# A fused scan, SwiGLU and softplus kernel: another preparation of its first four units

## The chip, the cores and the metric

The kernel runs on one core of one Trainium2 chip. The metric is the device time of one execution in microseconds (us). TensorE is called PE here, VectorE DVE, ScalarE ACT, GpSimd POOL; SP is the engine that issues nearly all transfers.

## The reference

A chunked linear-attention scan runs over 4 batches of 8 heads and 768 positions; its output (3072 tokens of 256 values) goes through a root-mean-square norm and a SwiGLU MLP of width 1536, and then through a softplus MLP of width 2048. All of it is float32.

```python
for c in range(nc):                       # 24 chunks of 32 positions
    cum = np.cumsum(la, axis=-1)
    L = np.exp(cum[:, :, :, None] - cum[:, :, None, :]) * causal
    M = np.einsum('bhin,bhjn->bhij', Cc, Bc) * L
    y[:, :, sl] = M @ xc + (Cc @ state) * np.exp(cum)
    state = decay_full * state + sum_j(Bc xc decay_from_j)
...
xn = x / rms * rms_g
x = ((g := xn @ w_gate) * sigmoid(g) * (xn @ w_val)) @ w_out     # 256 -> 1536 -> 256
h = x @ w_in
return softplus(h) @ w_out2                                      # 256 -> 2048 -> 256
```

## The kernel before

**Units.** The scan is cut into 24 units of 128 positions, one for each batch and stretch: units 0 to 3 are the first stretch of the four batches, 4 to 7 the second. A unit (function `unit`) first makes its decays: two DVE scans of 128x512 (line L505) that multiply up the values of `a`, which every partition must hold. For a "spread" unit PE copies them to all partitions with four small matmuls (`p<-Sm,ident`); for the others a transfer of 512 KB does it (`ab<-a_clip`, L465; units 2 and 3 of the first block use the tiles `xxh` and `xxl` as their decay buffers, so there the name is `xxh<-...`, `xxl<-...`). `a_clip` is a clipped copy of `a` that the kernel itself writes to DRAM at the start (L778). Then PE computes the scores (`a<-hw`), DVE multiplies them into the decays (L552, two of 128x512) and scales B (L525), and PE applies the result (`t<-xc`, `t<-ab,xc`; from unit 4 on also `a<-xc,Sm` for the carried state, for which DVE multiplies in the products of the decays, L519). ACT drains the output into `xxh` (squares) and `xxl`; `norm` averages the squares on PE (`p<-mean,xxh`), takes the root on POOL, spreads it with PE (`p<-ident,rs`), and DVE applies it (L661) and takes the rest after rounding (L306, 128x256).

**The MLPs.** Tokens go in 6 blocks of 512 (4 units). Each float32 product is made of three matmuls of 128x512: high weight times high value, high times low, low times high. `front1` makes one of 12 slices of the gate (`wg`) and of the value (`wv`), 6 matmuls each; ACT applies silu (L706), DVE multiplies (L710), ACT rounds (`hw`), DVE takes the rest (L306, `hw<-s,hw`); `back` multiplies the slice by `wo` (`t<-hw,woh`). The second MLP has 16 slices with `wi` and `wp`.

**Weights.** 34 chunks of 512 KB of packed weights arrive in three rotating buffers `wr`. Each needs an ACT conversion (`zz`, L389), a DVE shift and merge (L391), an ACT rounding to the high part (L394), and the rest, the low part: on DVE (L396), but for the first four chunks (`PE_RESTS`) by PE, two products with scaled identities (`p<-wr,wil` and, for instance, `p<-wgh,wil`) that ACT then copies out (L299).

**Order.** All operations are collected in a plan with a rank and a cost; `Plan.emit` then walks through time and always emits the operation that can start first, on any engine, with ties going to the lower rank. That fixes each engine's instruction order; on the chip every engine runs its list strictly in that order and waits by semaphores. 40 idle matmuls (`p<-mean`, "fillers") have the lowest rank after the first eight. Transfers on SP reuse eight semaphores in turn, so each also waits for the eighth one before it.

Of the kernel before, what the change touches and what calls it, by code (L numbers as in the profile page):

```python
# [13 lines left out]
ACTF = mybir.ActivationFunctionType  # L14
# [3 lines left out]
P = 128  # L18
# [5 lines left out]

BLOCKS = [4, 4, 4, 4, 4, 4]

NATIVE, SPREAD = 8, 4
NORMS = {0: [1, 1, 1, 1]}

EARLY, HEAD = 2, 2  # L30
# [6 lines left out]

LAT, DMA_LAT = 300, 500

ANY_ORDER = {}  # L40

PE_RESTS, REST_LEAD = 4, 6
F1 = 1536 // P
F2 = 2048 // P
KD = DM // P
# [17 lines left out]
class Plan:  # L63
# [48 lines left out]
    def emit(self):  # L112
# [57 lines left out]
        while len(order) < n:  # L170
            best = None
            for e in engines:
                able = []
                for i in cand[e]:
                    t = start(i, e)
                    if t is not None:
                        able.append((t, ops[i][1], i))
                while able:
                    t, rank, i = min(able)
                    if best is not None and t >= best[0]:  # L180
                        break
                    end = t + ops[i][0][e][0]

                    later = False
                    for e2, way in ops[i][0].items():
                        if e2 != e:
                            ns, t2 = way[0], start(i, e2)
                            t2 += sum(ops[j][0][e2][0] for j in cand[e2]
                                      if len(ops[j][0]) == 1 and ops[j][1] < rank and ready[j] <= t2)
                            later = later or t2 + ns < end  # L190
                    if not later:
                        best = (t, e, i)
                        break
                    able.remove((t, rank, i))
            if best is None:
                raise RuntimeError("no operation can run")
            t, e, i = best
            ns, fn, *shared = ops[i][0][e]
            for e2 in ops[i][0]:
                cand[e2].discard(i)  # L200
            end = t + ns
            if e == "pe":
                end = self.clock(t, ns, ops[i][4], ticks)
            if e in dma:

                dma[e] = max(t + 1100, dma[e]) + ns * (1.5 if e == "actq" else 1.0)
                end = dma[e] + DMA_LAT
                free[e] = t + 475
            else:
                free[e] = end  # L210
                if e == "pool":
                    port = end
            order.append(fn)
            for key, b in news[i]:
                slots[key].remove(min(slots[key]))
                taken[key].add(b.turn)
                while first[key] in taken[key]:
                    first[key] += 1
            for b in uses[i]:
                b.left -= 1  # L220
                b.rel = max(b.rel, end + self.latency)
                if not b.left:
                    slots[b.pool, b.tag].append(b.rel)
            for j, data in succ[i]:
                if data:
                    ready[j] = max(ready[j], end + (20 if list(ops[j][0]) == [e] else self.latency))
                left[j] -= 1
                if not left[j]:
                    enter(j)
# [5 lines left out]
def tile_ssd_then_swiglu_then_softplus_mlp(  # L235
# [34 lines left out]
    def f32(t):  # L270
        return t.bitcast(F32)
# [16 lines left out]
    def DVE(n, rank, fn, r=(), w=(), fast=False, port=True, ns=None):  # L288
        plan.op({"dve": (ns or dve_ns(n, fast), fn) + (("port",) if port else ())}, rank, r, w)
# [71 lines left out]
    for i in range(F2 // 2):  # L361
        chunks += [("wi", i), ("wp", i)]


    MINUS, minus = len(chunks) - 2, "minus"

    def scaled_ident():
        return W["wi"][1][:, F2 - 1]

    def weight(c):  # L370
        nm, i = chunks[c]
        b0 = blocks[0]
# [19 lines left out]
            op0=ALU.logical_shift_right, op1=ALU.bitwise_or), [raw, zk], [raw])  # L392
        h, l = (W[nm][s][:, 2 * i:2 * i + 2].rearrange("p a k f -> p (a k f)") for s in (0, 1))
        ACT(n, rank, lambda: act.activation(out=h, in_=r(), func=ACTF.Copy, scale=256.0), [raw], [(nm, i, 0)])  # L394
        if c >= PE_RESTS:
            DVE(n, rank, lambda: dve.scalar_tensor_tensor(out=l, in0=r(), scalar=256.0, in1=f32(h), op0=ALU.mult,  # L396
                op1=ALU.subtract), [raw, (nm, i, 0)], [(nm, i, 1)] + [minus] * (c == MINUS))
            return
        gp = pbuf("p", [P, 4 * P])

        def rest():
            mm(gp(), f32(scaled_ident()[:, 0]), r(), True, False)
            mm(gp(), scaled_ident()[:, 1], h, False, True)
        PE(1090, use - REST_LEAD, rest, [raw, (nm, i, 0), "ident", minus], [gp], 2560)
        COPY(n, rank, lambda: l, gp, [gp], [(nm, i, 1)], False)

    wp = []

# [32 lines left out]
    def unit(u):  # L441
# [83 lines left out]
                dve.tensor_tensor(out=ob, in0=ob, in1=lst.to_broadcast([P, NH, NS]), op=ALU.mult)  # L525
            DVE(128, rank[0], scale, [(abt, 0), (abt, 1), xbt], [(xbt, "b")])
        nxt(2)
        gps = [pbuf("a", [P, 4 * P]) for _ in range(2)]
        if nat:

            def scores():
# [229 lines left out]
    with tc.manual_schedule():  # L761
# [2 lines left out]
        ACT(384, -101, lambda: act.activation(  # L764
            out=ident4[:, P:4 * P].rearrange("p (o i) -> p o i", o=3),
            in_=ident.rearrange("p (o i) -> p o i", o=1).to_broadcast([P, 3, P]), func=ACTF.Copy), ["eye"], ["ident"])
        for k, m in enumerate((256.0, -1.0)):
            ACT(128, -50, lambda k=k, m=m: act.activation(out=scaled_ident()[:, k], in_=ident, func=ACTF.Copy, scale=m), ["ident"], [minus])

        def a_view(t):  # L770
            return t.rearrange("u o (h g i) -> (u o h) g i", g=2, i=P)

# [124 lines left out]
```

## Time and profile before

| | |
|---|---|
| median of 3 runs | 652.39 us (652.33 to 652.45) |
| the profiled execution: its time, its span | 651.48 us, 649.0 us |
| PE busy | 643.7 us, 99% of the span |
| DVE busy | 339.7 us, 52%; by tenths nearly full up to 130 us |
| ACT busy | 309.9 us, 48% |
| POOL busy | 24.6 us, 4% |

Before the first matmul of the MLP (`p<-xxh,wgh`, at 34.99 us) PE carries the first units and the fillers; from there to the end it carries the MLPs, with the later units in between. An operation that waits shows the engine and line that released it in brackets.

### The profile page before, as it was taken

How to read it: one execution, taken by the hardware profiler on the slowest of the kernel's cores; microseconds unless marked ns; L12 is line 12 of the kernel's file. 1: busy time of each engine (PE TensorE's matmuls, PEld its weight loads, DVE VectorE, ACT ScalarE, POOL GpSimd, SP SyncE). 2: the span in 40 equal slices, each digit the busy share in tenths (PEclk: the TensorE clock that was granted, in tenths of full speed). 3: DMA queues.
4: the chain of work that ended last, by engine and by line, in shares of the span. 5: the costliest groups of instructions: out<-in, count | busy, mean ns of one | idle time of the engine just before them, and what ended most of it. 6: DMA issues, size and time to landing. Idle time of an engine off the chain costs nothing.

```text
span 649.0 us, 9018 instructions
## 1 busy us (share of the span) xinstructions
PE 643.7 (99%) x3492; PEld 528.9 (81%) x3492; DVE 339.7 (52%) x566; ACT 309.9 (48%) x547; POOL 24.6 (4%) x32
## 2 busy tenths in 40 slices
PE   9999999999999999999999999999999999999997
PEld 7778888888888888888888888888888888887785
DVE  5988988876833237564324963423753422233321
ACT  4376657756355444233643433644432544433543
POOL 1210000000100001000001100000000000000000
PEclk9999999999999999999999999999999999999999
DMA  6786776574500015300323420141500000000000
GB/s 209 223 292 195 241 273 197 196 230 165 172 1 32 2 32 171 123 1 0 123 89 124 140 62 1 70 141 32 171 1 1 1 1 0 33 1 0 1 1 32
DMA packets 36777, 61.36 MB, mean 95 GB/s; under 512 B 3424, under 2 KB 18304, under 8 KB 36736
## 3 DMA queue, kind: packets, MB, share of 16 engines
q1 hardware_dynamic: 36304, 59.23, 28.0%
q10 hardware_dynamic: 432, 1.57, 0.7%
q8 instruction: 27, 0.44, 0.3%
q14 instruction: 14, 0.11, 0.1%
HBM read 47.58 MB, written 13.21 MB: 94 GB/s over the span
## 4 chain that ended last, share of the span: by engine, by line
PE 98%; ACT 0%; DVE 0%; issue 0%; DVEq 0%
PE p L268 55%; PE t L268 36%; PE a L268 8%; DVE hw L306 0%; ACT hw L299 0%; DVE xxl L751 0%; DVE s L710 0%; ACT s L722 0%; ACT xxh L299 0%; ACT s L756 0%; DVE mean L781 0%; DVE small L782 0%; DVEq L710 0%
## 5 line engine op out<-in xcount | busy, mean ns | idle before, releaser
L306 DVE TENSOR_TENSOR hw<-s,hw 128x512 fp32r<-128x512 f32 x162 | 113.5, 703 | 179.6 <-ACT hw L299 178.9
L299 ACT ACTIVATE hw<-s 128x512 fp32r<-128x512 f32 x162 | 101.9, 632 | 99.5 <-DVE s L710 76.8
L268 PE MATMUL t<-hw,wph 128*128 128x512 f32 x384 | 119.6, 392 | 0.2 <-DVE hw L306 0.2
L722 ACT ACTIVATE s<-p 128x512 f32<-128x512 f32 x96 | 56.9, 598 | 103.7 <-PE p L268 102.6
L710 DVE TENSOR_TENSOR s<-s,p 128x512 f32<-128x512 f32 x72 | 49.2, 683 | 72.7 <-PE p L268 65.4
L268 PEld LDWEIGHTS t<-hw,wph 128*128 128x128 f32 x384 | 71.3, 188 | 16.7 <-issue 1.2
L268 PE MATMUL t<-hw,woh 128*128 128x512 f32 x264 | 82.3, 392 | 0.4 <-DVE hw L306 0.2
L268 PE MATMUL p<-xxl,wih 128*128 128x512 f32 x192 | 74.9, 390 | 0.2 <-DVE xxl L751 0.2
L268 PE MATMUL p<-xxh,wih 128*128 128x512 f32 x192 | 75.0, 390 | 0.0
L268 PE MATMUL t<-hw,wpl 128*128 128x512 f32 x192 | 74.7, 389 | 0.0
L268 PE MATMUL p<-xxh,wil 128*128 128x512 f32 x192 | 74.7, 389 | 0.0
L706 ACT ACTIVATE s<-p 128x512 f32<-128x512 f32 x72 | 43.0, 597 | 62.9 <-PE p L268 61.5
L268 PEld LDWEIGHTS t<-hw,woh 128*128 128x128 f32 x264 | 49.2, 188 | 11.7 <-DVE hw L306 0.8
L268 PE MATMUL p<-xxh,wgh 128*128 128x512 f32 x144 | 57.1, 397 | 0.0
L268 PE MATMUL p<-xxh,wvh 128*128 128x512 f32 x144 | 57.0, 396 | 0.0
L268 PE MATMUL p<-xxl,wgh 128*128 128x512 f32 x144 | 56.2, 390 | 0.0
L268 PE MATMUL p<-xxh,wvl 128*128 128x512 f32 x144 | 56.1, 390 | 0.0
L268 PE MATMUL p<-xxl,wvh 128*128 128x512 f32 x144 | 56.1, 390 | 0.0
L268 PE MATMUL p<-xxh,wgl 128*128 128x512 f32 x144 | 56.1, 389 | 0.0
L505 DVE TENSOR_TENSOR_SCAN ab<-ab,ident 128x512 f32<-128x512 f32 x40 | 50.4, 1279 | 5.8 <-DMA ab<-a_clip 5.8
L268 PE MATMUL t<-hw,wol 128*128 128x512 f32 x132 | 51.4, 389 | 0.0
L268 PEld LDWEIGHTS p<-xxl,wih 128*128 128x128 f32 x192 | 36.1, 188 | 8.0 <-DVE xxl L751 0.7
(121 smaller groups left out, 782.1 us busy)
## 6 DMA issues: line engine op xcount, KB each, us to landing
wr<-in_w SPq DMA_DIRECT2D x31, 512.0 KB, 4.3
ab<-a_clip SPq DMA_DIRECT2D x20, 512.0 KB, 4.5
parts<-wr SPq DMA_DIRECT2D x16, 512.0 KB, 3.6
xc<-in_xc SPq DMA_DIRECT2D x20, 256.0 KB, 4.4
st<-parts SPq DMA_DIRECT2D x16, 256.0 KB, 3.1
cz<-parts SPq DMA_DIRECT2D x32, 128.0 KB, 3.8
out_y<-s SPq DMA_DIRECT2D x12, 256.0 KB, 2.9
wr<-in_bc SPq DMA_DIRECT2D x8, 256.0 KB, 3.3
```

The source lines that it names most:

```text
L268: pe.matmul(out=o, lhsT=l, rhs=r, start=start, stop=stop, skip_group_check=True)
L299: ways = {"act": (act_ns(n), lambda: act.activation(out=out(), in_=in_(), func=ACTF.Copy)), "dve": (dve_ns(n, sbuf), lambda: dve.tensor_co ...
L306: return lambda: eng.tensor_tensor(out=out(), in0=in_(), in1=f32(hi()), op=ALU.subtract)
L505: DVE(512, rank[0], lambda t=t, d=d: dve.tensor_tensor_scan(out=t(), data0=d(), data1=ident4, initial=0.0, op0=ALU.mult, op1=ALU.add), dk ...
L706: ACT(n, rank - EPI, lambda: act.activation(out=s()[:, 0:n], in_=ps[0]()[:, 0:n], func=ACTF.Silu), [ps[0]], [s, "table"] if new_table else ...
L710: DVE(n, rank - EPI, lambda: dve.tensor_tensor(out=s()[:, 0:n], in0=s()[:, 0:n], in1=ps[1]()[:, 0:n], op=ALU.mult), [s, ps[1]], [s], port= ...
L722: ACT(n, rank - EPI, lambda: act.activation(out=s()[:, 0:n], in_=hp()[:, 0:n], func=ACTF.Softplus), [hp], [s, "table"] if new_table and f ...
```

## The change

Four things change. `SPREAD` goes from 4 to 2: the decays of units 2 and 3 come by transfer from `a_clip`. The scores of units 1 and 3 go into banks of the pool `p` of PSUM, which the MLP uses, instead of `a`. `PE_RESTS` is gone: the low parts of all chunks are made by DVE, and the scaled identities are not built. And `emit` gets a rule: while an operation of rank below -50 could start on an engine, no other is put there unless it ends at most 150 ns (planned) after that start.

```diff
--- before.py
+++ after.py
@@ -24,7 +24,9 @@
 
 BLOCKS = [4, 4, 4, 4, 4, 4]
 
-NATIVE, SPREAD = 8, 4
+NATIVE, SPREAD = 8, 2
+
+SCORES_P = (1, 3)
 NORMS = {0: [1, 1, 1, 1]}
 
 EARLY, HEAD = 2, 2
@@ -37,9 +39,9 @@
 
 LAT, DMA_LAT = 300, 500
 
+URGENT, HELD_UP = -50, 150
+
 ANY_ORDER = {}
-
-PE_RESTS, REST_LEAD = 4, 6
 F1 = 1536 // P
 F2 = 2048 // P
 KD = DM // P
@@ -175,6 +177,10 @@
                     t = start(i, e)
                     if t is not None:
                         able.append((t, ops[i][1], i))
+
+                urgent = min((t for t, rank, i in able if rank < URGENT), default=None)
+                if urgent is not None:
+                    able = [c for c in able if c[1] < URGENT or c[0] + ops[c[2]][0][e][0] <= urgent + HELD_UP]
                 while able:
                     t, rank, i = min(able)
                     if best is not None and t >= best[0]:
@@ -361,12 +367,6 @@
     for i in range(F2 // 2):
         chunks += [("wi", i), ("wp", i)]
 
-
-    MINUS, minus = len(chunks) - 2, "minus"
-
-    def scaled_ident():
-        return W["wi"][1][:, F2 - 1]
-
     def weight(c):
         nm, i = chunks[c]
         b0 = blocks[0]
@@ -392,17 +392,8 @@
             op0=ALU.logical_shift_right, op1=ALU.bitwise_or), [raw, zk], [raw])
         h, l = (W[nm][s][:, 2 * i:2 * i + 2].rearrange("p a k f -> p (a k f)") for s in (0, 1))
         ACT(n, rank, lambda: act.activation(out=h, in_=r(), func=ACTF.Copy, scale=256.0), [raw], [(nm, i, 0)])
-        if c >= PE_RESTS:
-            DVE(n, rank, lambda: dve.scalar_tensor_tensor(out=l, in0=r(), scalar=256.0, in1=f32(h), op0=ALU.mult,
-                op1=ALU.subtract), [raw, (nm, i, 0)], [(nm, i, 1)] + [minus] * (c == MINUS))
-            return
-        gp = pbuf("p", [P, 4 * P])
-
-        def rest():
-            mm(gp(), f32(scaled_ident()[:, 0]), r(), True, False)
-            mm(gp(), scaled_ident()[:, 1], h, False, True)
-        PE(1090, use - REST_LEAD, rest, [raw, (nm, i, 0), "ident", minus], [gp], 2560)
-        COPY(n, rank, lambda: l, gp, [gp], [(nm, i, 1)], False)
+        DVE(n, rank, lambda: dve.scalar_tensor_tensor(out=l, in0=r(), scalar=256.0, in1=f32(h), op0=ALU.mult, op1=ALU.subtract),
+            [raw, (nm, i, 0)], [(nm, i, 1)])
 
     wp = []
 
@@ -525,7 +516,7 @@
                 dve.tensor_tensor(out=ob, in0=ob, in1=lst.to_broadcast([P, NH, NS]), op=ALU.mult)
             DVE(128, rank[0], scale, [(abt, 0), (abt, 1), xbt], [(xbt, "b")])
         nxt(2)
-        gps = [pbuf("a", [P, 4 * P]) for _ in range(2)]
+        gps = [pbuf("p" if u in SCORES_P else "a", [P, 4 * P]) for _ in range(2)]
         if nat:
 
             def scores():
@@ -764,9 +755,6 @@
         ACT(384, -101, lambda: act.activation(
             out=ident4[:, P:4 * P].rearrange("p (o i) -> p o i", o=3),
             in_=ident.rearrange("p (o i) -> p o i", o=1).to_broadcast([P, 3, P]), func=ACTF.Copy), ["eye"], ["ident"])
-        for k, m in enumerate((256.0, -1.0)):
-            ACT(128, -50, lambda k=k, m=m: act.activation(out=scaled_ident()[:, k], in_=ident, func=ACTF.Copy, scale=m), ["ident"], [minus])
-
         def a_view(t):
             return t.rearrange("u o (h g i) -> (u o h) g i", g=2, i=P)
```

**DVE, first units** (`SCALAR_TENSOR_TENSOR` at L505 and L496 is a scan; `ab<-p` reads decays spread by PE). Before, from unit 0's first scan to unit 2's:

```order
L505 SCALAR_TENSOR_TENSOR ab<-p,ident_68 128x512 x2
L391 SCALAR_TENSOR_TENSOR wr<-wr,zz_73 128x512
L525 TENSOR_TENSOR xc<-xc,ab 128x128
L505 SCALAR_TENSOR_TENSOR ab<-p,ident_68 128x512
L552 TENSOR_TENSOR ab<-ab,a 128x512
L505 SCALAR_TENSOR_TENSOR ab<-p,ident_68 128x512
L552 TENSOR_TENSOR ab<-ab,a 128x512
L525 TENSOR_TENSOR xc<-xc,ab 128x128
L391 SCALAR_TENSOR_TENSOR wr<-wr,zz_74 128x512
L797 TENSOR_SCALAR s<-s 96x256
L799 SCALAR_TENSOR_TENSOR s<-s,cst_sb 96x128 x2
```

Now, over the same stretch of the program:

```order
L496 SCALAR_TENSOR_TENSOR ab<-p,ident_68 128x512 x2
L516 TENSOR_TENSOR xc<-xc,ab 128x128
L543 TENSOR_TENSOR ab<-ab,a 128x512
L496 SCALAR_TENSOR_TENSOR ab<-p,ident_68 128x512 x2
L543 TENSOR_TENSOR ab<-ab,a 128x512
L516 TENSOR_TENSOR xc<-xc,ab 128x128
L496 SCALAR_TENSOR_TENSOR xxh<-xxh,ident_68 128x512
L543 TENSOR_TENSOR ab<-ab,p 128x512
L496 SCALAR_TENSOR_TENSOR xxh<-xxh,ident_68 128x512
L543 TENSOR_TENSOR ab<-ab,p 128x512
L516 TENSOR_TENSOR s<-s,xxh 128x128
L543 TENSOR_TENSOR xxh<-xxh,a 128x512
```

The shifts of weights (L391) and the products of the decays (L797, L799) have moved behind the units, and unit 2's first scan, which now reads what a transfer brought (`xxh<-xxh`), stands ahead of all of unit 1's score products (`ab<-ab,p`) and of unit 3.

**DVE, around the first slices of the MLP.** Before, from the last rest of the norm (`xxl<-xxl,xxh`) to the rest of the first slice (`hw<-s,hw`):

```order
L306 TENSOR_TENSOR xxl<-xxl,xxh 128x2x128
L591 SCALAR_TENSOR_TENSOR S<-S,xc,a 128x64
L391 SCALAR_TENSOR_TENSOR wr<-wr,zz_74 128x512
L552 TENSOR_TENSOR ab<-ab,a 128x512
L391 SCALAR_TENSOR_TENSOR wr<-wr,zz_73 128x512
L552 TENSOR_TENSOR ab<-ab,a 128x512
L710 TENSOR_TENSOR s<-s,p 128x512
L396 SCALAR_TENSOR_TENSOR wvl<-wr,wvh 128x512
L505 SCALAR_TENSOR_TENSOR ab<-ab,ident_68 128x512
L306 TENSOR_TENSOR hw<-s,hw 128x512
```

Now, the last twelve rows up to the same rest of the first slice:

```order
L391 SCALAR_TENSOR_TENSOR wr<-wr,zz_73 128x512
L496 SCALAR_TENSOR_TENSOR ab<-ab,ident_68 128x512
L395 SCALAR_TENSOR_TENSOR wol<-wr,woh 128x512
L516 TENSOR_TENSOR xc<-xc,ab 128x128
L496 SCALAR_TENSOR_TENSOR ab<-ab,ident_68 128x512
L543 TENSOR_TENSOR ab<-ab,a 128x512 x2
L496 SCALAR_TENSOR_TENSOR ab<-ab,ident_68 128x512
L701 TENSOR_TENSOR s<-s,p 128x512
L516 TENSOR_TENSOR xc<-xc,ab 128x128
L391 SCALAR_TENSOR_TENSOR wr<-wr,zz_74 128x512
L701 TENSOR_TENSOR s<-s,p 128x512
L312 TENSOR_TENSOR hw<-s,hw 128x512
```

One rest of weights (`wol`), two shifts, three scans (unit 4's second and unit 5's two) and unit 4's score products (`ab<-ab,a`) now stand between the norm and the first slice's rest. Before, all of that but shifts was done ahead of the norm's last rest, and unit 5's score products and one scan of unit 6 stood here.

**PE, just ahead of the MLP.** Before:

```order
L268 MATMUL p<-wgh,wil 128x512
L268 MATMUL p<-wr,wil 128x512
L268 MATMUL p<-wvh,wil 128x512
L268 MATMUL p<-ident_68,rs 128x128
L268 MATMUL a<-xc,Sm 128x128 x2
L268 MATMUL a<-xc 32x64 x4
L268 MATMUL a<-ab,xc 32x128 x8
L268 MATMUL p<-wr,wil 128x512
L268 MATMUL p<-woh,wil 128x512
L268 MATMUL p<-xxh,wgh 128x512
```

Now:

```order
L274 MATMUL p<-mean 128x512 x3
L274 MATMUL p<-mean,xxh 128x1 x2
L274 MATMUL p<-mean 128x512 x3
L274 MATMUL p<-ident_68,rs 128x128
L274 MATMUL p<-mean 128x512
L274 MATMUL p<-ident_68,rs 128x128
L274 MATMUL a<-hw 128x128 x8
L274 MATMUL p<-xxh,wgh 128x512
```

The products for the weights' rests are gone, unit 4's output (`a<-xc,Sm` and on) has moved behind the first two slices, and the scores of unit 4 (`a<-hw`) are the last thing ahead of the MLP. Behind it, 24 matmuls of two slices now run straight up to the first `t<-hw,woh`; unit 4's output, unit 5's scores and unit 5's output all come after that one, where before they came ahead of it.

## Rows read from the trace of the kernel before

**Rows 1.** The page, busy times, granted clock and the chain that ended last

```profile
PE 643.7 (99%) x3492; PEld 528.9 (81%) x3492; DVE 339.7 (52%) x566; ACT 309.9 (48%) x547; POOL 24.6 (4%) x32
...
PEclk9999999999999999999999999999999999999999
...
PE 98%; ACT 0%; DVE 0%; issue 0%; DVEq 0%
```

**Rows 2.** Timeline of PE, start: start us, duration us, what

```profile
0.92 4.19 PE L268 MATMUL p<-mean 128*128 128x512 f32 x10 [0.92 <-DVE small L782]
...
9.50 4.07 PE L268 MATMUL p<-mean 128*128 128x512 f32 x17
...
16.18 1.97 PE L268 MATMUL p<-Sm,ident 96*128 96x256 f32 x8
17.99 0.39 PE L268 MATMUL p<-ident,rs 128*128 128x128 f32 x2
```

**Rows 3.** Timeline of PE, rests of weights, first slices, unit 5, first back

```profile
33.75 1.17 PE L268 MATMUL p<-wr,wil 128*128 128x512 f32 x2
...
34.99 0.40 PE L268 MATMUL p<-xxh,wgh 128*128 128x512 f32 x1
...
36.45 1.16 PE L268 MATMUL a<-hw 16*128 16x128 f32 x16
...
39.03 1.06 PE L268 MATMUL p<-wr,wil 128*128 128x512 f32 x2
...
40.16 0.61 PE L268 MATMUL a<-xc,Sm 128*128 128x128 f32 x4
...
41.39 0.50 PE L268 MATMUL p<-xxh,wgh 128*128 128x512 f32 x1
...
44.24 0.62 PE L268 MATMUL t<-hw,woh 128*128 128x512 f32 x2
```

**Rows 4.** Timeline of DVE, the first units

```profile
12.54 0.28 DVE L525 TENSOR_TENSOR xc<-xc,ab 128x128 f32<-128x128 f32 x1
12.74 0.68 DVE L391 SCALAR_TENSOR_TENSOR wr<-wr,zz 128x512 int32<-128x512 int32 x1
14.76 0.29 DVE L797 TENSOR_SCALAR s<-s 96x256 f32<-96x256 f32 x1 [1.33 <-DMA s<-in_ab]
...
15.74 0.66 DVE L391 SCALAR_TENSOR_TENSOR wr<-wr,zz 128x512 int32<-128x512 int32 x1
16.32 1.27 DVE L552 TENSOR_TENSOR ab<-ab,a 128x512 f32<-128x512 f32 x2
17.52 2.33 DVE L505 TENSOR_TENSOR_SCAN xxh<-p,ident 128x512 f32<-128x512 f32 x2
19.76 0.39 DVE L661 TENSOR_TENSOR xxl<-xxl,p 128x256 f32<-128x256 f32 x1
...
26.47 0.41 DVE L306 TENSOR_TENSOR xxl<-xxl,xxh 128x256 fp32r<-128x256 f32 x1
26.81 0.68 DVE L552 TENSOR_TENSOR xxl<-xxl,a 128x512 f32<-128x512 f32 x1
...
34.29 0.41 DVE L306 TENSOR_TENSOR xxl<-xxl,xxh 128x256 fp32r<-128x256 f32 x1
```

**Rows 5.** Timeline of SP's queue, issue of the copy of a and of the next transfers

```profile
6.62 0.35 SPq L778 DMA_DIRECT2D a_clip<-Sm  x1
...
11.12 0.42 SPq L486 DMA_DIRECT2D s<-in_xc  x1
```

**Rows 6.** Line L778, write of a_clip: issue to landing

```profile
DMA to landing us min/median/max: 5.3/5.3/5.3
```

**Rows 7.** Line L465, decays by transfer, 6 issued before 120 us

```profile
DMA to landing us min/median/max: 3.9/5.3/8.0
```

**Rows 8.** Line L465, decays by transfer, 14 issued after 120 us

```profile
DMA to landing us min/median/max: 3.3/4.0/6.5
```

**Rows 9.** Transfers issued from 15 to 30 us: count, size, median us to landing

```profile
prods<-s SPq DMA_DIRECT2D x2, 768.0 KB, 6.1
```

**Rows 10.** Timeline of ACT, a weight chunk's conversion

```profile
35.68 0.78 ACT L389 ACTIVATE zz<-wr 128x512 f16<-128x512 bf16 x1
```

## The prediction, made before the changed kernel had run

> **What bounds the kernel now.** I read the page first. PE is busy for 99% of the span, the chain that ended last lies 98% on PE, and the granted clock stands at its upper level in every slice [rows 1]. So the time is the moment at which PE starts the MLP, plus the matmuls that are left, plus whatever PE has to wait for. The matmuls of the MLPs are the same before and after. What can move is the stage ahead of the MLP and the first slices, so next I read the timelines of PE and DVE for the first 46 us. PE is full there too, but 40 of its matmuls are fillers (10 take 4.19 us at the start, 17 take 4.07 us later [rows 2]), so its 99% says nothing there. DVE is the engine to watch. Its rows follow each other without a gap from 17.52 us to the last rest of the norm, which ends at 34.29 + 0.41 = 34.70 us [rows 4]; PE starts the MLP at 34.99 us [rows 3].
>
> **What PE loses and gains.** Two spread units go: one takes from 16.18 to 17.99, 1.81 us [rows 2], so 3.6 us. Four rests go: one from 33.75 to 34.99, one from 39.03 to 40.16, 1.24 and 1.13 us [rows 3], so 4.7 us for four. That is 8.3 us less PE work, and none of it is gained by itself, since PE waits for DVE either way. ACT loses four copies and two small scalings, which lie beside other work and are costed at nothing; were ACT the bound, each copy would be a gain. The new banks for the scores of units 1 and 3 let these scores start earlier, but their products with the decays stand in DVE's list behind unit 2's first scan, so they gain nothing either. The new rule in `emit` has no cost of its own: it acts through the order, which is priced below, and so do the rests that are now DVE's (three of the four stand in the chain below).
>
> **What DVE must do now, and from when.** Unit 2's first scan now waits for a transfer, and behind it in DVE's list stand unit 1's score products, and so everything else. When does it land? The copy of `a` is issued at 6.62 us and lands 5.3 us later [rows 5, 6], at 11.92. SP's list has its last loads ahead of it issued by 11.12 + 0.42 [rows 5], so the transfer of unit 2 goes out at about 11.95. Transfers of this kind took 3.3 to 6.5 us, median 4.0, when few others ran [rows 8], and 3.9 to 8.0, median 5.3, in the crowded first 120 us [rows 7]. Only one load of 192 KB is still under way ahead of it, so I take 4.0: it lands at 15.95 and the scan starts at 16.0. DVE will have finished what it can at about 12.2: before, it was through with the same work of units 0 and 1 at 12.74 [rows 4], and one shift of 0.6 us is no longer ahead of that. DVE so stands idle for nearly 4 us. PE, whose next work (unit 1's output) waits for those score products, stands too.
>
> From that scan to the rest of the first slice (`hw<-s,hw`), which the first `t<-hw,woh` needs, DVE has 41 instructions. I price each by the distance from its start to the next start where rows stand back to back [rows 4]. Eight scans (units 2 and 3, unit 4, unit 5) at (19.76 - 17.52)/2 = 1.12 make 8.96 us. Eleven of 128x512 (eight score products, two gate products and the rest itself) at (17.52 - 16.32)/2 = 0.60 make 6.60. Seven shifts and rests of weights at 16.32 - 15.74 = 0.58 make 4.06. Eight norm products and rests of 256 columns at 26.81 - 26.47 = 0.34 make 2.72. Four small scalings at 12.74 - 12.54 = 0.20 make 0.80. The clip and the two short scans for the products of decays take 15.74 - 14.76 = 0.98 together.
>
> That is 24.1 us. To this come waits inside the chain (a rest must wait for ACT's rounding, a norm for POOL's root). The nearest measure is the same kind of chain before: from 17.52 to 34.70 DVE ran 28 instructions (the first and the last of them in [rows 4]), 8 scans, 6 score products, 8 of 256 columns and 6 small ones, 8.96 + 3.60 + 2.72 + 1.20 = 16.5 us by the same prices, in 17.2: 0.7 us of waits. I take 0.8. So DVE is through at 16.0 + 24.1 + 0.8 = 40.9 us.
>
> **What PE does meanwhile.** The last rest of the norm comes after 5 scans, 6 score products, 4 weight operations, 8 of 256 columns, 2 scalings and the 0.98: 16.0 + 5.60 + 3.60 + 2.32 + 2.72 + 0.40 + 0.98 + 0.8 = 32.4. The first MLP matmul can go a little earlier, at about 31.8: some 3 us ahead of 34.99. The second matmul needs that rest and goes at 32.4; 23 are left of the 24 of two slices, and twelve took 44.24 - 41.39 = 2.85 us [rows 3], so PE is through with them at 32.4 + 23 x 0.24 = 37.8. Then it stands until the rest at 40.9. That wait of 3.1 us takes the place of the lead.
>
> **The sum.** Before, PE began the first `t<-hw,woh` at 44.24 with unit 4's and unit 5's outputs and unit 5's scores behind it [rows 3]. Now it gets past its first high matmul, 0.2 us of work, by 40.9, and still owes one output for each of the two units (41.39 - 40.16 = 1.23 us, twice) and the scores (1.1 us): 3.56 - 0.2. That makes it level with the old 44.24 at 40.9 + 3.3 = 44.2. I add 0.3 us for the scores of unit 5, which must now wait until ACT has drained both `a` banks of unit 4. The difference is 44.5 - 44.24 = +0.3 us. Against the profiled execution that is 651.48 + 0.3 = 651.8; the median of the runs shown lies 0.9 us above the profiled one, so the forecast for the median is **652.7 us**. A measurement of this kernel can tell about 0.2% (1.3 us) from no change, so this is "no change".
>
> The bounds: with the transfer at 3.3 us the sum is -0.4 us, at 5.3 us it is +1.6, each microsecond of landing being one of the end. The Trainium skill, "DMA: Bandwidth & Descriptors", section "Anatomy of one DMA", gives about 2.0 us plus bytes over 436 GB/s for one DMA of another queue kind, so 3.2 us for 512 KB; by that the sum would be -0.5 us. The least row, 3.3, agrees with it, the median does not.
>
> **Rivals.** In the first, slower, the clock falls. PE now stands twice for some 3 us, near 16 to 20 and near 38 to 41. Before, the granted clock stayed up in every slice of the page [rows 1]; but out of the idleness at the start PE needed 4.19 us for ten fillers, where ten of the later ones take 2.4 us [rows 2]: one stretch at the lower level cost 1.8 us. Behind the first stand PE has room for that. Behind the second its matmuls are the bound again, so a fall there decides: 652.7 + 1.8 = 654.5. The Trainium skill, "TensorE: Matmul & The Clock Gate", Part 1, says that the clock drops to 1.2 GHz after an idle stretch and comes back after sustained work; no row here shows a drop. Chance 0.24.
>
> In the second, also slower, a transfer is later. The two transfers of the decays' products (768 KB each, 6.1 us to land [rows 9]) now go out one right behind the other after the products on DVE, at about 16.0 + 12.0 + 0.4 = 28.4, and SP's list has weight chunk 4 behind them. That chunk's ACT conversion of 0.78 us [rows 10] stands in ACT's list ahead of the first slices' rounding, and its shift two places ahead of the deciding rest on DVE, where it is due at 39.1. So it decides once chunk 4 lands after 38.3; or else the first transfer takes 5.3 us or more. I price either at 1.5 us: 654.2. Chance 0.14.
>
> In the third, faster, the lead stays. If DVE were not what the first slices wait for, PE would go on at 37.8 and, with 3.56 us still owed, be level with the old 44.24 at 41.4: 2.9 us earlier, 649.5. For that DVE's chain would have to be 3 us shorter than the sum; 1.6 us shorter would already count as faster. The prices are those of the same instructions, so it would take a landing near 3.3 us, no waits at all, and something else. Against it speaks also that DVE ran just such a chain at these prices before [rows 4]. Chance 0.14.
>
> **How the numbers follow.** The likeliest case has 0.48; its own range is 651.6 to 653.6. The two slower rivals make 0.38, the faster one 0.14. The range of 8 in 10 reaches from 651.0, which leaves out most of the lead, to 655.0, which leaves out the clock and a late transfer together.
>
> **What the changed profile would show.** DVE's first transfer-fed scan (`xxh<-xxh,ident`) starts at 15.3 to 17.3, with DVE idle ahead of it from 12.2, released by a transfer. The first `p<-xxh,wgh` comes at 31 to 33 us. The first `t<-hw,woh` pair is split or late, PE idle ahead of it for 2 to 3.5 us and released by DVE `hw` or ACT `hw`, near 40.9. Wrong would be: no such idle stretch (then the lead stays), or fillers and slices at 0.42 us per matmul behind it (then the clock fell), or the wait ended by ACT's conversion of chunk 4.

## The result, and the profile after

The changed kernel takes 657.23 us (median of 22 executions, 652.97 to 660.24), the kernel before on the same chip 652.42 us (22, 651.75 to 659.84); the ratio is 1.0054, 95% interval 1.0036 to 1.0072. It is slower by half a per cent, 4.5 us above the forecast of 652.7 and outside its range. The profiled execution took 656.6 us (span 654.6), 5.1 us more than the profiled one of before.

The page first, for [rows 1]: busy time of PE, the granted clock in 40 slices of 16 us, and the chain that ended last.

```profile
PE 644.1 (98%) x3464; PEld 528.2 (81%) x3464; DVE 342.0 (52%) x570; ACT 306.5 (47%) x541; POOL 24.3 (4%) x32
...
PEclk9589999999999999999999999999999999999999
...
PE 94%; DMA 3%; DVE 2%; issue 1%; ACT 0%; SPq 0%; POOL 0%; DVEq 0%
```

PE's share fell by only one point, but the clock row has a 5 in its second slice and an 8 in its third where before there were nines, and a transfer has 3% of the chain. The windows say more (start:end; total us; busy us and count of PE, PEld, DVE, ACT, POOL; granted clock; DMA share; GB/s):

```profile
17.00:18.00 1.00, 0.00 (x0) 0.00 (x0) 0.75 (x1) 0.00 (x0) 0.00 (x0) 0.89 0.90 305
18.00:31.00 13.00, 10.67 (x73) 7.70 (x73) 10.84 (x19) 3.72 (x14) 1.83 (x3) 0.50 0.43 147
...
38.00:42.00 4.00, 4.00 (x12) 3.09 (x11) 4.00 (x6) 1.18 (x2) 0.00 (x0) 0.57 0.94 341
```

The row from 17 to 18 us, at 0.89 with PE idle throughout, has the fall. From 18 to 31 us the granted clock is 0.50 (1.2 GHz of 2.4), though PE is busy for 10.67 of these 13 us; from 38 to 42 it is at that level for most of the time again. PE's timeline, for [rows 2, 3], has the stands (in brackets the wait and who ended it):

```profile
19.10 0.65 PE L274 MATMUL t<-ab,xc 128*32 128x128 f32 x8 [2.43 <-DVE ab L543]
20.82 0.66 PE L274 MATMUL t<-ab,xc 128*32 128x128 f32 x8 [1.06 <-DVE ab L543]
21.64 0.80 PE L274 MATMUL p<-ident,rs 128*128 128x128 f32 x2 [0.17 <-POOL rs L622]
22.09 2.05 PE L274 MATMUL p<-mean 128*128 128x512 f32 x4
...
24.72 2.07 PE L274 MATMUL p<-hw 16*128 16x128 f32 x16
...
36.51 0.50 PE L274 MATMUL p<-xxh,wgh 128*128 128x512 f32 x1 [0.35 <-ACT xxh L305]
...
45.90 0.50 PE L274 MATMUL t<-hw,woh 128*128 128x512 f32 x1 [0.86 <-DVE hw L312]
```

PE stands for 2.43 us, then 1.06, both times for unit 1's score products on DVE (`ab`, L543). The third wait, for POOL's root, is 0.17 us. Behind that, four fillers take 2.05 us (17 took 4.07 at the upper level [rows 2]) and the sixteen score matmuls of unit 3 (`p<-hw`) 2.07, where sixteen took 1.16 [rows 3]. DVE's timeline, for [rows 4]:

```profile
12.09 0.28 DVE L516 TENSOR_TENSOR xc<-xc,ab 128x128 f32<-128x128 f32 x1
17.25 1.22 DVE L496 TENSOR_TENSOR_SCAN xxh<-xxh,ident 128x512 f32<-128x512 f32 x1 [4.88 <-DMA xxh<-a_clip]
...
26.82 0.69 DVE L543 TENSOR_TENSOR xxl<-xxl,p 128x512 f32<-128x512 f32 x1 [1.17 <-PE p L274]
28.41 0.42 DVE L652 TENSOR_TENSOR xxl<-xxl,p 128x256 f32<-128x256 f32 x1 [0.90 <-PE p L274]
...
34.65 0.42 DVE L652 TENSOR_TENSOR xxl<-xxl,p 128x256 f32<-128x256 f32 x1 [1.60 <-PE p L274]
...
45.16 0.68 DVE L312 TENSOR_TENSOR hw<-s,hw 128x512 fp32r<-128x512 f32 x1
```

DVE waits 4.88 us for unit 2's transfer, where nearly 4 were forecast, and later 1.17, 0.90 and 1.60 us for PE, which was not. The deciding rest is done at 45.16 + 0.68 = 45.84, where I had 40.9. One engine whose list the prediction did not price is POOL; ACT, which makes what the root reads, waits for a load too:

```profile
20.30 0.73 POOL L506 TENSOR_TENSOR Sm<-S,cst_sb 128x256 f32<-128x256 f32 x1 [16.80 <-DMA small<-in_rms_g]
21.04 0.55 POOL L622 TENSOR_TENSOR rs<-rs,small 128x1 f32<-128x1 f32 x1
```

```profile
20.27 0.62 ACT L593 ACTIVATE xxl<-t,small 128x128 f32<-128x128 f32 x2 [6.11 <-DMA small<-in_rms_g]
```

POOL's list now has unit 4's product with `cst_sb` ahead of the first root; by the rows below `cst_sb` (issued at 13.29) landed at about 20.1 us and `rms_g` at 20.25, so the two loads end together. Before it was the other way round:

```profile
17.23 0.55 POOL L631 TENSOR_TENSOR rs<-rs,small 128x1 f32<-128x1 f32 x1 [13.73 <-ACT rs L630]
...
22.60 0.74 POOL L515 TENSOR_TENSOR Sm<-S,cst_sb 128x256 f32<-128x256 f32 x1 [1.08 <-PE p L268]
```

And the chain of work that ended last (start us, us, what) passes just there and not through DVE's wait, though by a margin of only 0.17 us: that is all that PE waited for the root once unit 1's output was done.

```profile
13.76 6.49 DMA small<-in_rms_g
...
20.30 0.73 POOL Sm L506
...
21.04 0.56 POOL rs L622
...
21.64 6.73 PE p L274 x30
```

The 1 KB load of `rms_g`, issued at 13.76, was under way for 6.49 us. Both that load and `cst_sb` now go out on SP's queue behind the two transfers of 512 KB. Transfers issued from 0 to 30 us (count, KB each, median us to landing), after and then before:

```profile
cst_sb<-in_cst SPq DMA_DIRECT2D x1, 128.5 KB, 6.8
...
s<-in_ab SPq DMA_DIRECT2D x1, 96.0 KB, 6.2
...
small<-in_rms_g SPq DMA_DIRECT2D x1, 1.0 KB, 6.5
```

```profile
cst_sb<-in_cst SPq DMA_DIRECT2D x1, 128.5 KB, 2.5
...
s<-in_ab SPq DMA_DIRECT2D x1, 96.0 KB, 2.2
...
small<-in_rms_g SPq DMA_DIRECT2D x1, 1.0 KB, 2.5
```

Each of the three small loads takes about 4 us longer from issue to landing than before, whatever its size. Whether the order in the queue does that, or DMA engines that are busy anyway (a share of 0.90 from 17 to 18 us), these rows do not tell.

Time goes with the clock from execution to execution. The five of the 22 with a mean granted clock of 0.995 or 0.996 took 652.97 to 655.44 us, median 653.9; the thirteen below 0.99 took 655.8 to 660.2, median 658.0. The kernel before has such executions too, on the chips of the experiments more of them (651.6 to 664 us), so each ratio below, always to the kernel before on the same chip, has a wide interval, and of its 28 to 35 executions there the three to six that lie over 1.5% above the fastest are left out of it. Mean clocks are given beside times.

### The profile page after: what moved, and what is told of

Read it like the earlier page. It is cut to its first block, busy times and chain, and to the rows that moved or that the text cites. A ratio compares the mean times of both kernels' runs of the same rounds, so it can differ in the third digit from the quotient of the medians.

```text
span 654.6 us, 8963 instructions
## 1 busy us (share of the span) xinstructions
PE 644.1 (98%) x3464; PEld 528.2 (81%) x3464; DVE 342.0 (52%) x570; ACT 306.5 (47%) x541; POOL 24.3 (4%) x32
## 4 chain that ended last, share of the span: by engine, by line
PE 94%; DMA 3%; DVE 2%; issue 1%; ACT 0%; SPq 0%; POOL 0%; DVEq 0%
PE p L274 51%; PE t L274 35%; PE a L274 7%; DMA small<-in_rms_g 1%; DMA a_clip<-Sm 1%; DMA wr<-in_w 1%; DVE hw L312 0%; DVE ab L496 0%; DMA ident<-in_eye 0%; ACT hw L305 0%; DVE wr L391 0%; DVE s L701 0%; DVE ab L543 0%; SPq L456 0%; DVE xxl L652 0%
## 5 line engine op out<-in xcount | busy, mean ns | idle before, releaser
L496 DVE TENSOR_TENSOR_SCAN ab<-ab,ident 128x512 f32<-128x512 f32 x40 | 50.6, 1286 | 5.9 <-DMA ab<-a_clip 5.9
```

The source lines that it names most:

```text
L496: DVE(512, rank[0], lambda t=t, d=d: dve.tensor_tensor_scan(out=t(), data0=d(), data1=ident4, initial=0.0, op0=ALU.mult, op1=ALU.add), dk ...
```

## The experiments

In the code below `...` stands for what is left out, and constants that a kernel names are written as their values; the comment in the code of `early_clip` is not in the kernel.

**Which part of the change.** Two kernels, one with all but the transfers, one with the transfers alone.

```diff
-NATIVE, SPREAD = 8, 2     # changed kernel
+NATIVE, SPREAD = 8, 4     # spread4
```

> The changed kernel with the decays of units 2 and 3 copied by PE again; score banks, weight rests on DVE and the rule in emit stay changed. Theory: nothing on DVE waits for a transfer before unit 4, PE does not stand, the clock stays up: 651.5 to 654 us with little spread. Rival 1 (weight rests on DVE) and a rival that blames the score banks or the rule: 656 to 658 us, since all of these stay.

Measured: 653.67 us (12 executions, 651.26 to 657.27), ratio 0.9998 (0.9970 to 1.0027). Score banks, rests on DVE and the rule together cost nothing that can be measured (the interval ends 1.8 us up); this rival falls. That PE would not stand was not borne out: in its profile, of its slowest execution (657.27 us), PE stood for 1.79 us for POOL's first root, and the clock was at 0.52 from 31 to 38 us.

```diff
-NATIVE, SPREAD = 8, 4     # kernel before
+NATIVE, SPREAD = 8, 2     # spread2_alone
```

> The kernel before with only the decays of units 2 and 3 by transfer; everything else as before. Theory: DVE waits for the transfer landing at about 17.2 us, PE stands, the clock falls: 656 us or more, with a large spread and a mean clock under 0.99. Rival 1 and the rival of score banks and rule: 652 to 653 us, as the kernel before.

Measured: 660.39 us (6; 658.33 to 662.49), ratio 1.0102 (1.0069 to 1.0136), mean clocks 0.983 to 0.990. So the loss comes with `SPREAD`, that is with the transfers for units 2 and 3. That the rest of the change takes some of it back is likely and not shown: the two intervals just meet, on different chips. Here too POOL's list has the product with `cst_sb` ahead of the first root, so that swap comes with `SPREAD`, and in this profile it alone makes the stand: DVE waits 3.09 us for the transfer while PE has other work, and PE then stands for the root.

```profile
18.76 0.72 POOL L515 TENSOR_TENSOR Sm<-S,cst_sb 128x256 f32<-128x256 f32 x1 [15.26 <-DMA small<-in_rms_g]
```

```profile
20.96 0.49 PE L268 MATMUL p<-ident,rs 128*128 128x128 f32 x2 [2.77 <-POOL rs L631]
```

**Is it the clock?** One kernel fills the stand in the changed kernel, another makes a stand in the kernel before.

```diff
             for s in range(2):
+                if u == 1:
+                    for _ in range((11, 5)[s]):
+                        filler()
                 intra(s)
```

> The changed kernel with 16 more idle matmuls, 11 and 5, just ahead of the two halves of unit 1's output, where PE stood for 2.4 and 1.1 us while DVE waited for unit 2's transfer. Nothing else moves. Theory: the stand lets PE's clock fall, and half-speed scores of unit 3 and norms then hold DVE up for 3.7 us; with PE kept at work there the granted clock stays at its upper level from 17 to 31 us and the time is that of the late transfer alone, 652.5 to 654.5 us, with little spread from run to run. Rival 1 (the weight rests on DVE and its longer chain are the cost) and rival 2 (the late transfer by itself, the clock being a bystander): 656 to 658 us as before.

Measured: 654.76 us (12; 653.05 to 658.34), ratio 1.0018 (0.9988 to 1.0047), mean clock 0.992 to 1.000. Its windows, and DVE's last row of the chain:

```profile
17.00:31.00 14.00, 13.60 (x138) 10.14 (x137) 12.83 (x22) 5.74 (x22) 4.24 (x4) 1.00 0.51 159
31.00:44.00 13.00, 9.17 (x49) 6.65 (x49) 12.08 (x21) 6.46 (x12) 1.29 (x2) 1.00 0.82 252
44.00:47.00 3.00, 3.00 (x9) 2.37 (x8) 2.96 (x7) 2.26 (x4) 0.00 (x0) 0.53 0.52 175
```

```profile
23.41 0.42 DVE L656 TENSOR_TENSOR xxl<-xxl,p 128x256 f32<-128x256 f32 x1 [0.93 <-PE p L275]
...
32.35 0.42 DVE L656 TENSOR_TENSOR xxl<-xxl,p 128x256 f32<-128x256 f32 x1 [0.92 <-PE p L275]
...
42.84 0.69 DVE L313 TENSOR_TENSOR hw<-s,hw 128x512 fp32r<-128x512 f32 x1
```

The clock stays up through the first stand. DVE waits for PE for 0.93 + 0.92 us instead of 3.67 (its scan had started at 16.42), and the rest is done at 43.53. Behind the second stand the clock still falls (0.53 from 44 to 47). The median is 0.3 us above what I had expected, and 2.5 to 2.9 below the changed kernel's, on other chips.

```diff
-            PE(213, ..., filler, ...)
+            PE(213, ..., filler if i not in range(10, 29) else (lambda: None), ...)
```

> The kernel before with 19 of its 40 idle matmuls left out (those between 9.5 and 16 us), so that PE stands there for some 4 us; no transfer, no DVE instruction and no order changes. Theory: the clock falls behind that stand and half-speed PE work delays DVE: 654 to 658 us, mean clock below 0.995. Rival (the late transfer alone, or the weight rests on DVE): 652.4 us as before, since neither is touched.

Measured: 658.03 us (12; 653.73 to 660.28), ratio 1.0054 (1.0026 to 1.0083), mean clock 0.986 to 0.989 in eleven of twelve.

```profile
9.00:13.00 4.00, 2.23 (x24) 1.34 (x22) 4.00 (x7) 2.13 (x3) 0.00 (x0) 0.97 0.80 254
13.00:29.00 16.00, 15.62 (x92) 12.68 (x92) 9.87 (x18) 3.89 (x13) 1.19 (x3) 0.50 0.79 238
30.00:60.00 30.00, 30.00 (x239) 22.97 (x228) 27.11 (x46) 18.90 (x41) 3.44 (x4) 1.00 0.58 189
```

```profile
18.94 1.22 DVE L506 TENSOR_TENSOR_SCAN xxh<-p,ident 128x512 f32<-128x512 f32 x1 [0.54 <-PE p L269]
...
24.30 0.69 DVE L553 TENSOR_TENSOR xxh<-xxh,a 128x512 f32<-128x512 f32 x1 [1.92 <-PE a L269]
...
27.17 1.22 DVE L506 TENSOR_TENSOR_SCAN xxl<-p,ident 128x512 f32<-128x512 f32 x1 [1.25 <-PE p L269]
```

Leaving idle matmuls out, and nothing else, costs what the whole change costs. PE stands in parts of 9 to 13 us, then runs at 0.50 for 16 us while busy for 15.62 of them, and DVE, whose list is the same as before, waits for PE at these and other places. This shows that a stand of PE alone, through the clock, is dear here.

**The changed kernel once more.** 

> The changed kernel as it is, once more, so that the others have it beside them on the same chip. Theory: where PE stands for unit 2's transfer the clock falls in most executions; time follows the mean clock, 656 to 660 us where the clock is below 0.99 and 653 to 654.5 us where it stays above 0.994. A rival by which the clock is a bystander expects no such bond between the two.

Measured: 657.70 us (12; 653.57 to 661.19), ratio 1.0038 (1.0004 to 1.0072); the six below 0.99 took 656.9 to 661.2, the two above 0.994 took 653.6 and 655.4. That is the bond between clock and time again. Its profile is of an execution of 655.0 us:

```profile
20.54 0.65 PE L274 MATMUL t<-ab,xc 128*32 128x128 f32 x8 [3.45 <-DVE ab L543]
```

```profile
33.49 0.42 DVE L652 TENSOR_TENSOR xxl<-xxl,p 128x256 f32<-128x256 f32 x1 [0.92 <-PE p L274]
...
43.98 0.69 DVE L312 TENSOR_TENSOR hw<-s,hw 128x512 fp32r<-128x512 f32 x1
```

```profile
19.00:25.00 6.00, 3.21 (x22) 2.03 (x23) 5.90 (x9) 1.81 (x8) 1.28 (x2) 0.50 0.69 208
```

The scan started at 18.68, 1.43 us later than in the first profile, and PE stood for longer (3.45 us). But the clock was back at its upper level by 26 us, after about half as long; DVE waited for PE for 0.92 us instead of 3.67, and the rest was done at 44.67 instead of 45.84. So in these two executions of one kernel the time goes with how long the clock is down, not with the length of the stand. Why the clock came back sooner here is not shown.

**Both stands filled.** Besides the 16 idle matmuls, 12 into the bank of the first `t<-hw,woh`, just ahead of it.

```diff
             def prod(m=m, o=acc[t][m]):
                 a, b = (W[wt][s][:, f, m] for s in (0, 1))
+                if (layer, t, f, m) == (1, 0, 0, 0):
+                    idle(o, 12)
```

> The kernel with the first stand filled (16 idle matmuls) and besides 12 idle matmuls just ahead of the first product of the first slice, the second stand of 1.7 and 0.8 us behind which the clock had still fallen for 2.9 us. Theory: the mean granted clock is above 0.998 in nearly all executions, and 1.0 to 1.5 us more are saved: 652.5 to 653.8 us. Rival (the late transfer alone, the clock a bystander): 654.8 us as with the first stand filled.

Measured: 654.40 us (12; 652.40 to 657.26), ratio 0.9971 (0.9941 to 1.0002), mean clock 0.997 to 1.000 in all twelve. The clock came about as expected, the time did not and is nearer to the rival's 654.8: in its profile, of its slowest execution, the twelve ended 1.1 us after the rest for which they were to wait, since PE had reached them late. There the fixed number of idle matmuls cost what it overran. Against the changed kernel on the same chip (`after_again`) the filled stands gain 3.3 us; what is left is 1.6 us above the 19 executions of the kernel before there with a mean clock of 0.997 or more (median 652.8).

**A planner that knows of late transfers**, then with 12 idle matmuls ahead of unit 3's scores.

```diff
-LAT, DMA_LAT = 300, 500
+LAT, DMA_LAT = 300, 2500
...
             def scores():
+                if u == 3:
+                    for _ in range(12):
+                        filler()
```

> The changed kernel with the planner's latency of a transfer (DMA_LAT) raised from 500 to 2500 ns, so that its order of work no longer puts unit 2's first scan ahead of work that is ready. Theory: DVE works while the transfer is on its way, unit 1's score products and output come before the scan, PE does not stand for long before 20 us, the clock stays up there: 651 to 654 us. Rival 1 (weight rests) and a rival of score banks: 656 to 658 us.

Measured: 653.81 us (12; 651.83 to 655.72), ratio 0.9983 (0.9955 to 1.0012). The time is as expected, but not for the reason given: PE still stood for 3.19 us ahead of unit 3's scores, the clock fell behind it, and little of DVE's chain waited for that stretch (0.92 us).

> The kernel with the planner's latency of all transfers at 2500 ns (653.8 us, with rms_g ahead of the two transfers on SP), and 12 idle matmuls ahead of unit 3's scores, where PE had stood for 3.2 us and the clock had fallen for 6.8 us. Theory: that fall goes, mean clock from 0.992 to 0.996 or more, 651.5 to 653.2 us. Rival (the clock a bystander): 653.8 us.

Measured: 653.39 us (12; 652.15 to 656.10), ratio 1.0005 (0.9982 to 1.0027), mean clock 0.989 to 0.997. That fall is gone from the profile, another came at 31 us; 0.4 us is too little to tell.

**Four misses.** `late4000_keep20` adds to the planned landing of units 2 and 3 alone, and fills two stands:

```diff
-                    ready[j] = max(ready[j], end + (20 if list(ops[j][0]) == [e] else self.latency))
+                    ready[j] = max(ready[j], end + (4000 if i in self.late else 0) + (20 if list(ops[j][0]) == [e] else self.latency))
...
         def spread():
+            if (t, o0) == (0, 0):
+                idle(wp[0], 20)
```

> The changed kernel with one more thing known to the planner: the two transfers for units 2 and 3 are taken to land 4 us later, so that it lists unit 1's products, unit 2's scores and a weight shift ahead of the first scan that waits; and 20 and 3 idle matmuls keep PE at work in the two stands. Theory: DVE's head-of-line wait no longer holds up unit 1, the clock stays up, 650.5 to 652.5 us, level with the kernel before or a little faster. Rival (the weight rests on DVE are the cost): 655 us or more, since they all stay on DVE.

Measured: 656.90 us (12; 654.60 to 659.33), ratio 1.0041 (1.0014 to 1.0067). DVE's wait had only moved: after its first two scans it waited 3.80 us for PE's spread of the first root, PE for POOL.

`early_clip` moves two issues up in the finished order, `early_clip_l2` besides takes the two transfers to be 2000 ns late:

```diff
+        for mark, fns in self.ahead:   # clip and write of a_clip ahead of unit 2's loads, its transfer ahead of unit 3's
+            for fn in fns:
+                order.remove(fn)
+            k = order.index(self.marks[mark])
+            order[k:k] = fns
         for fn in order:
             fn()
```

> The changed kernel with the write of a_clip issued ahead of unit 2's loads of B and C, and the transfer of unit 2's decays ahead of unit 3's; PE, DVE and ACT keep their lists. Theory: a_clip goes out at about 4.9 us in place of 7.4, unit 2's first scan starts 2 to 3 us earlier (14.5 to 15.5 us), PE's first stand of 2.4 us all but goes and with it the fall of the clock behind it, and DVE's chain to the first slice's rest ends 4 to 6 us earlier: 650 to 652.5 us, at a mean clock above 0.993. Rival (the weight rests on DVE, the score banks or the rule are the cost): 656 us or more, since all of these stay.

Measured: 657.64 us (12; 655.09 to 660.87), ratio 1.0024 (0.9993 to 1.0055). `a_clip` went out at 4.71 but took 7.6 us to land, so unit 2's transfer went out at 12.36 as ever; the loads of B and C behind `a_clip` went out only at 7.86 and later, and PE stood 3.38 us for POOL's root:

```profile
23.81 0.80 PE L280 MATMUL p<-ident,rs 128*128 128x128 f32 x2 [3.38 <-POOL rs L634]
```

> The same earlier transfers, and a planner that takes the transfers of units 2 and 3 to land 2 us later, so that unit 1's score products and output come ahead of the first scan that waits. Theory: still less stands behind the transfer; 650 to 652 us. What could spoil it: the transfer of rms_g, behind which ACT and so the first norm wait, held up the run with 4 us; if it is that, 654 us or more with DVE waiting for PE's spread of the root.

Measured: 660.62 us (12; 658.94 to 666.31), ratio 1.0085 (1.0048 to 1.0122): nearly the spoiler that I had named, a wait of 3.45 us for POOL's root; but POOL waited for `cst_sb`, until 19.27, and not for `rms_g`.

`spread4_keep` is `spread4` with 8 fillers at the same place, the first root's spread:

> The kernel with units 2 and 3 spread by PE again, with 8 idle matmuls ahead of the first spread of a root, where PE had stood for 1.8 us and the clock had fallen behind it. Theory: fewer falls of the clock, 651.5 to 653 us (651.3 to 651.8 us were its executions at a mean clock of 0.999). Rival (the clock a bystander): 653.7 us as without them.

Measured: 654.12 us (12; 652.27 to 655.10), ratio 0.9974 (0.9941 to 1.0007), against 653.67 without them on another chip: no gain is shown.

**The second holder: loads that POOL and ACT wait for.**

```diff
-        LOAD(20, -1, lambda: nc.sync.dma_start(out=g_sb, in_=rms_g), ["g"])
+        plan.op({"actq": (80.0, lambda: act.dma_start(out=g_sb, in_=rms_g))}, -140, ["ident"], ["g"])
```

> The changed kernel with the load of rms_g (1 KB) issued by ACT behind its three weight loads instead of by SP behind the two transfers of units 2 and 3; every other list stays. In the changed kernel ACT stood until 20.3 us for it. Theory A (unit 2's transfer, by DVE's wait, sets the stand): PE still stands until 19 us, the clock still falls, 655.5 to 657.5 us. Theory B (rms_g, by ACT and the first root, sets when PE has work again): PE's work comes back by 18 us, 652.5 to 654.5 us.

Measured: 657.90 us (12; 652.34 to 660.21), ratio 1.0060 (1.0032 to 1.0089). ACT no longer waited, and PE still stood for POOL's root, which now waited for `cst_sb`:

```profile
21.35 0.72 POOL L506 TENSOR_TENSOR Sm<-S,cst_sb 128x256 f32<-128x256 f32 x1 [17.85 <-DMA cst_sb<-in_cst]
22.04 1.47 POOL L622 TENSOR_TENSOR rs<-rs,small 128x1 f32<-128x1 f32 x1
```

So `rms_g` alone is not the holder. Next `cst_sb` goes to ACT's queue as well, and both loads in the planner's versions.

```diff
-        LOAD(128, -10, lambda: nc.sync.dma_start(out=cst_sb[:, 0:DM + 1], in_=cst), ["cst"], ["a_clip"])
+        plan.op({"actq": (512.0, lambda: act.dma_start(out=cst_sb[:, 0:DM + 1], in_=cst))}, -139, ["ident"], ["cst"])
```

> The changed kernel with the loads of rms_g and of cst_sb (128.5 KB) both issued by ACT behind its three weight loads; DVE, PE and POOL keep their lists. With rms_g alone moved, PE still stood for 2.3 us for the first root, because POOL's list has unit 4's product with cst_sb ahead of it and cst_sb had landed at 21.3 us. Theory A (unit 2's transfer alone is enough): POOL's wait goes, PE still stands until 19 us for DVE, the clock still falls, 655 to 657.5 us. Theory B (cst_sb, by POOL, is what makes the stand long enough): 652.5 to 654.5 us, clock 0.994 or more.

Measured: 654.85 us (12; 653.13 to 660.53), ratio 1.0011 (0.9969 to 1.0053).

```profile
15.01 0.73 POOL L506 TENSOR_TENSOR Sm<-S,cst_sb 128x256 f32<-128x256 f32 x1 [11.51 <-DMA s<-in_xc]
16.55 0.55 POOL L622 TENSOR_TENSOR rs<-rs,small 128x1 f32<-128x1 f32 x1 [0.81 <-ACT rs L621]
```

```profile
19.60 0.43 PE L274 MATMUL t<-ab,xc 128*32 128x128 f32 x8 [1.89 <-DVE ab L543]
```

The first root is done at 17.1 us instead of 21.6, PE no longer waits for it, and stands only for DVE. Five of twelve executions keep a mean clock of 0.995 or more and take 653.1 to 654.2 us; of the changed kernel it was seven of 34, with `rms_g` alone moved one of twelve. In the others, the profiled one among them, the clock still fell. The median is 3 us lower than with `rms_g` alone moved, on the same chip, but the two intervals overlap. Its profile is of an execution of 656.8 us, no faster than the profiled one of the changed kernel, where POOL's root had held PE for only 0.17 us; and PE's work ahead of the stand comes about 1 us later in it, which shortens DVE's part of the stand too (1.89 us instead of 2.43). How much of the loss is POOL's wait and how much DVE's is not shown.

> The kernel whose planner takes the transfers of units 2 and 3 to land 4 us later, with the idle matmuls in its stands, which came out at 656.9 us, and besides rms_g issued by ACT. There DVE had waited 3.8 us for PE's first root, and that for rms_g. If that second transfer is what had spoiled it: DVE's wait of 3.8 us goes, the fall of the clock at 24.9 us goes, 651.5 to 653.5 us. If the weight rests or the order itself are the cost: 655.5 us or more still.

Measured: 656.39 us (12; 654.41 to 657.61), ratio 1.0025 (0.9997 to 1.0053): a miss, POOL again waited for a load until 21.58.

> The kernel whose planner takes the two transfers to land 4 us later, with idle matmuls in its stands and rms_g issued by ACT (656.4 us), and besides cst_sb issued by ACT. There DVE waited 2.65 us for PE's spread of the first root, PE for POOL, POOL for a load. If POOL's list is the holder: PE's first root is spread by about 17 us, DVE's wait for it goes, 652 to 654 us. If the order itself or the weight rests are the cost: 656 us still.

Measured: 654.38 us (12; 653.60 to 655.70), ratio 0.9998 (0.9967 to 1.0029). POOL's first root starts at 16.24 instead of 22.26, and 2.0 us are gone, on the same chip: with this order POOL's list was a holder. The 20 idle matmuls, put in for the old wait, now stand ahead of the root's spread themselves, so DVE still waits 2.40 us for it.

> The kernel with the planner's latency of transfers at 2500 ns and 12 idle matmuls ahead of unit 3's scores (653.4 us), and besides the loads of rms_g and cst_sb issued by ACT. SP's list is then two loads shorter ahead of the later ones. Theory: 651 to 652.8 us, a little faster than the kernel before on the same chip; if these loads did not matter there, 653.4 us again.

Measured: 653.71 us (12; 652.74 to 655.63), ratio 1.0001 (0.9974 to 1.0028): a miss, these loads did not matter there, where POOL's list has the root first. No version is shown to be faster than the kernel before.

## Why the prediction was wrong

**The step that failed** is in the first rival: "Behind the first stand PE has room for that." I had the fall of the clock as a rival of 0.24, but put it behind the second stand and priced it at 1.8 us, one stretch at the lower level. It came in the first stand, lasted 13 us, and PE had no room: its scores and norms of that stretch are on DVE's path. The sum shows it. DVE's chain ran from 17.25 to 45.84, 28.59 us; less the 3.67 us of waits for PE that is 24.92, and I had 24.1 + 0.8 = 24.9. So the prices of the 41 instructions, with what I had added for waits, cover the chain without PE. The forecast of +0.3, with 1.25 for the later start and 3.67 for the waits, gives +5.2; the profiled executions differ by 5.1. The same sum for `after_again`, 0.3 + 2.68 + 0.92, gives +3.9 where 3.5 was measured.

Not all of the 3.67 us is the clock's. Where the clock stayed up, or was back sooner, DVE still waited for PE for 1.85 us (`keep_clock`) and 0.92 (`after_again`). So by these two profiles the clock's part is about 1.8 to 2.75 us, and the 0.8 us for waits inside the chain was too small by 0.9 to 1.85 even without it.

**A mis-sized term** is the start of the scan, 16.0 in the prediction and 17.25 in the trace. `a_clip` went out 0.74 us later than before (7.36, [rows 5]) and landed in 5.0 us instead of 5.3; the transfer went out at 12.43 where I had 11.95, and took 4.8 us where I took 4.0. In the profiles of `keep_clock`, `keep_both` and `after_again`, which issue their transfers in the same order, the scan began at 16.42, 18.34 and 18.68.

**A step that was missing**: the order of POOL's list and the loads behind the transfers. I read SP's list for what stands ahead of unit 2's transfer, not for what stands behind it: `cst_sb`, `rms_g` and the second copy of `a`. Their 4 us, with POOL's swapped order, put the first spread of a root at 21.64. In the changed kernel's profile that is a second holder only 0.17 us behind the first; in other kernels it was the longer stand (2.77 us in `spread2_alone`, 2.31 in `g_act`, 3.38 in `early_clip`), and `g_act` and `late4000_keep20`, which dealt with one holder alone, showed no gain.

**What held, and what did not.** DVE's idle stretch ahead of a transfer-fed scan, released by a transfer, from 12.4 us; PE standing with it; a split first pair of `t<-hw,woh`, and the deciding wait on DVE's rest: these came. The lead did not: the first `p<-xxh,wgh` came at 36.51, 1.5 us later than before, where I had 31 to 33, and PE then stood for only 0.86 us ahead of the pair's second half, where I had 2 to 3.5. That the clock staying up leaves about no change is borne out in part: the executions of the changed kernel at 0.995 or more have a median of 653.9 us, 1.2 above the forecast and 1.5 above the kernel before, about the 0.3 and the 1.25 of the later start. Rival 2 (a later transfer) did not decide: the first transfer took 4.8 us and not 5.3, and weight chunk 4, for which ACT waited until 42.14, did land after 38.3, but DVE was later too and came to its shift only at 43.94:

```profile
42.14 0.80 ACT L389 ACTIVATE zz<-wr 128x512 f16<-128x512 bf16 x1 [2.45 <-DMA wr<-in_w]
```

The weight rests on DVE cost nothing that shows (`spread4`).

The Trainium skill, "TensorE: Matmul & The Clock Gate", Part 1, says that the clock drops to 1.2 GHz after an idle stretch and comes back after sustained work. The drop is now shown, by the windows of after and by `before_stand`; as for the return, PE was busy there for 15.62 of 16 us at the lower level, so by these rows work alone does not tell when it comes back. I had weighed that rule and given the drop the wrong place.

## What to carry to other kernels

Where PE is kept busy with idle matmuls, price a new stand not by its length but by what PE's work behind it costs at half speed (7 to 16 us of it in these profiles), and ask who waits for that work. Small loads issued behind a large transfer landed later here: list them, and who waits for each, POOL and ACT included. When one holder of a stand is taken away and nothing is gained, look in the chain for the next one before giving up the theory.

## What the runs showed of the hardware

The clock stayed at its lower level for 16 us while PE was busy for 15.62 of them (`before_stand`). On SP's queue three loads of 1 to 128.5 KB took 2.2 to 2.5 us with none of the 512 KB transfers just ahead of them (before) and 6.2 to 6.8 us behind two of them (after), regardless of size. The 1 KB of `rms_g` took 7.6 us on the other queue, behind ACT's three weight loads (`g_act`); it landed earlier only because it was issued earlier.
